# The last row tile's 512 output columns in two groups, and its last store in two halves

## The chip, the cores and the metric

The kernel runs on one core of one Trainium2 chip. The metric is device time in microseconds (us) of one execution. Before the change three executions took 163.49, 163.81 and 164.55 us; the median is 163.81.

## What is computed

A gated feed-forward layer: with x of 2048 x 640, w_gate and w_up of 640 x 1536, and w_down of 1536 x 640, all in bf16,

```python
def reference(x, w_gate, w_up, w_down):
    g = _silu(x @ w_gate)
    u = x @ w_up
    return (g * u) @ w_down
```

## The kernel before

The 2048 rows of x go through in four blocks of 512 (`sb`). For each block and each of twelve slices of 128 of the inner 1536 columns (`fc`), TensorE (PE) makes the gate and the up product in two PSUM tiles (`proj`, L192, five matmuls each), ScalarE (ACT) takes the silu of one (L212), and VectorE (DVE) multiplies it by the other into `aT` (L213), which holds the inner activations with the inner dimension on the partitions.

Then the block's output is made. The 640 output columns are split at `DA` = 512. The last 128 columns come first, transposed (`po_t`, L263, 512 rows wide, turned back by DVE at L274 and stored by ACT's queue at L276); in the last block this covers only the first three row tiles. The first 512 columns follow in four row tiles of 128 rows (`j` = 0 to 3): twelve matmuls of 512 columns each accumulate in `po_a` (L288), ACT casts the tile to bf16 (`ot`, L296), and SP issues the store (L301). In the very last row tile (`sb` = 3, `j` = 3, called `last`) the remaining 128 columns are made straight, not transposed: twelve matmuls of 128 columns into `po_b` (L305), a cast by DVE into `ot_b` (L313), and a store issued by ACT (L314).

`po_a` has two PSUM slots and `ot` three buffers, so a row tile waits for the cast of the tile two before it, and its cast for the store of the tile three before it. Beside this DVE works through 96 dot products for the last four rows (`row_dots`, L145); `do_dots` spreads them over the kernel, and `row_tail` at the first row tile of the last block finishes them, so none are left in the last row tile.

The Tile framework places the waits. On DVE and SP the program order is kept as it is written (`keep_order`); on ACT and PE it comes out in program order at the end as well. `_trim` takes away the barriers at the end: SP alone waits there for every semaphore (L394), two per EVENT_SEMAPHORE instruction and the last one on a DRAIN, and then clears them.

Of the kernel before, what the change touches and what calls it, by code (L numbers as in the profile page):

```python
# [10 lines left out]
def _body(  # L11
# [8 lines left out]
    nc = tc.nc  # L20
    P = nc.NUM_PARTITIONS
    f32 = mybir.dt.float32
    bf16 = mybir.dt.bfloat16
# [3 lines left out]
    B, S0, D = x.shape  # L27
# [3 lines left out]
    out2 = out.rearrange("b s d -> (b s) d")  # L31

    KD = D // P
    KF = F // P
    S_BLK = 512
    NSB = S // S_BLK
    SUB = S_BLK // P
    DA = 512
# [4 lines left out]
    ROW_J = 0  # L43
# [5 lines left out]
    outp = ctx.enter_context(tc.tile_pool(name="outp", bufs=3))  # L49
    psum = ctx.enter_context(  # L50
        tc.tile_pool(name="psum", bufs=2, space=bass.MemoryType.PSUM)
    )
# [6 lines left out]
    wd_sb = consts.tile([P, KF, D], bf16)  # L59
    aT = consts.tile([P, KF, S], bf16)  # L60
# [62 lines left out]
    def turn_x(sb):  # L123
        s_sl = slice(sb * S_BLK, (sb + 1) * S_BLK)
        nc.sync.dma_start_transpose(out=xT[:, :, s_sl], in_=xt_v[s_sl])

    def turn_w(dst, src):
        for a in range(0, KF, WT_STEP):
            nc.sync.dma_start_transpose(
                out=dst[:, a : a + WT_STEP, :], in_=src[:, a : a + WT_STEP, :]  # L130
            )
# [3 lines left out]
        out=x_row[:],  # L135
        in_=x2[S - T : S, :].rearrange("t d -> (t d)").partition_broadcast(P),
# [19 lines left out]
    def row_tail():  # L156
        for _ in dots:
            pass
        nc.scalar.activation(row_s[:], row_g[:], ACT.Silu)
        nc.vector.tensor_tensor(  # L160
            out=aT[:, :, S - T : S], in0=row_s[:], in1=row_u[:], op=ALU.mult
        )
# [3 lines left out]
    def do_dots(n):  # L166
        for _ in range(n):
            next(dots, None)
# [21 lines left out]
    def proj(ps, w_sb, fc, sb, c0, c1, cols=lambda ap: ap):  # L190
        for kd in range(KD):
            nc.tensor.matmul(  # L192
                cols(ps[:, c0:c1]),
                lhsT=w_sb[:, kd, fc * P : (fc + 1) * P],
                rhs=cols(xT[:, kd, sb * S_BLK + c0 : sb * S_BLK + c1]),
                start=(kd == 0),
                stop=(kd == KD - 1),
            )
# [4 lines left out]
    def gu_tiles():  # L203
        pg = psum.tile([P, S_BLK], f32, tag="gu", name="pg", bufs=4)
        pu = psum.tile([P, S_BLK], f32, tag="gu", name="pu", bufs=4)
        return pg, pu

    def gate(pg, pu, sb, fc, n_s):

        s0 = sb * S_BLK  # L210
        sg = work.tile([P, S_BLK], f32, name="sg")
        nc.scalar.activation(sg[:, 0:n_s], pg[:, 0:n_s], ACT.Silu)  # L212
        nc.vector.tensor_tensor(  # L213
            out=aT[:, fc, s0 : s0 + n_s], in0=sg[:, 0:n_s], in1=pu[:, 0:n_s], op=ALU.mult
        )
# [31 lines left out]
    for sb in range(NSB):  # L247
        n_s = S_BLK if sb < NSB - 1 else S_BLK - T
        for fc in range(KF):
            if sb == 0 and fc < 2:  # L250
                continue
            pg, pu = gu_tiles()
            proj(pg, wg_sb, fc, sb, 0, n_s)
            proj(pu, wu_sb, fc, sb, 0, n_s)
            gate(pg, pu, sb, fc, n_s)
            if sb > 0 and fc < KF - 2:
                do_dots(2)


        n_t = (SUB if sb < NSB - 1 else SUB - 1) * P  # L260
        po_t = psum.tile([P, n_t], f32, tag="po_b", name="po_t")
        for kf in range(KF):
            nc.tensor.matmul(  # L263
                po_t[:],
                lhsT=wd_sb[:, kf, DA:D],
                rhs=aT[:, kf, sb * S_BLK : sb * S_BLK + n_t],
                start=(kf == 0),
                stop=(kf == KF - 1),
            )
        ot_t = outp.tile([P, n_t], bf16, name="ot_t")  # L270
        ot_q = outp.tile([P, n_t], bf16, name="ot_q")
        nc.scalar.copy(ot_t[:], po_t[:])  # L272
        do_dots(3)
        nc.vector.transpose(out=ot_q[:], in_=ot_t[:])  # L274
        for q in range(P // Q):
            nc.scalar.dma_start(  # L276
                out=out2[
                    sb * S_BLK : sb * S_BLK + n_t, DA + q * Q : DA + (q + 1) * Q
                ].rearrange("(i r) c -> r i c", r=Q),
                in_=ot_q[q * Q : (q + 1) * Q, :].rearrange("r (i c) -> r i c", c=Q),  # L280
            )

        for j in range(SUB):
            s0 = sb * S_BLK + j * P
            last = sb == NSB - 1 and j == SUB - 1
            po_a = psum.tile([P, DA], f32, tag="po_a", name="po_a")
            for kf in range(KF):
                nc.tensor.matmul(  # L288
                    po_a[:],
                    lhsT=aT[:, kf, s0 : s0 + P],  # L290
                    rhs=wd_sb[:, kf, 0:DA],
                    start=(kf == 0),
                    stop=(kf == KF - 1),
                )
            ot = outp.tile([P, DA], bf16, name="ot")
            nc.scalar.copy(ot[:], po_a[:])  # L296
            if 0 < j:
                do_dots(3)
            if sb == NSB - 1 and j == ROW_J:
                row_tail()  # L300
            nc.sync.dma_start(out=out2[s0 : s0 + P, 0:DA], in_=ot[:])  # L301
            if last:
                po_b = psum.tile([P, D - DA], f32, tag="po_b", name="po_b")
                for kf in range(KF):
                    nc.tensor.matmul(  # L305
                        po_b[:],
                        lhsT=aT[:, kf, s0 : s0 + P],
                        rhs=wd_sb[:, kf, DA:D],
                        start=(kf == 0),
                        stop=(kf == KF - 1),  # L310
                    )
                ot_b = outp.tile([P, D - DA], bf16, name="ot_b")
                nc.vector.tensor_copy(out=ot_b[:], in_=po_b[:])  # L313
                nc.scalar.dma_start(out=out2[s0 : s0 + P, DA:D], in_=ot_b[:])  # L314
        if sb == 0:
            turn_x(2)
            turn_w(wuT, wut_v)
            turn_x(3)
# [72 lines left out]
def kernel(tc, *args):  # L391
    _body(tc, *args)
    tc.close()
    tc.compile()  # L394
    _trim(tc.nc)
# [30 lines left out]
```

## Time and profile before

| what | value |
|---|---|
| median of three executions | 163.81 us |
| the profiled execution: its span, first to last instruction (the page gives it no other time) | 163.0 us |
| PE busy | 159.9 us, 98% |
| DVE busy | 111.7 us, 69% |
| ACT busy | 42.6 us, 26% |
| granted TensorE clock | 1.000 |
| matmul spacing at 512 columns | 0.216 us |
| last matmul ends | 160.94 us |
| last DMA issue (`ot_b`) | 161.28 us |
| cast of 128x512 by ACT | 585 ns |
| cast of 128x128 by DVE | 290 ns |

Times in the profile count from the first instruction. The median is 0.81 us longer than the span; the span leaves out what the device does before the first and after the last instruction. A DMA is issued by an engine's queue (SPq, ACTq) and then takes a while to land, which is when its semaphore is complete; the time of a landing is not busy time of any engine. Lines are called L and a number; DMA issues have a queue, a count, the KB of each and the median us from issue to landing.

### The profile page before, as it was taken

Reading aid. Unit: us, or ns where it says so; the run is one execution under the profiler, and the core shown is the slowest. Engines: PE = TensorE matmul, PEld = TensorE weight load, DVE = VectorE, ACT = ScalarE, POOL = GpSimd, SP = SyncE. Lnnn points to the kernel's source line nnn. Section 1 sums busy time; section 2 is a strip of 40 time slices with the busy share of each in tenths; the row PEclk is TensorE's granted clock in tenths of the full one; section 3 lists DMA queues with packets and bytes.
Section 4 is the critical chain, followed back from the end, with each engine's and each line's share of the span. In section 5 each row is a group of like instructions: output and inputs, shape, how many; then the busy total and the mean of one; then the engine's idle time right before and its main releaser. Section 6 shows DMA issues by size and latency. Waiting matters only on the chain.

```text
span 163.0 us, 2109 instructions
## 1 busy us (share of the span) xinstructions
PE 159.9 (98%) x787; PEld 77.1 (47%) x799; DVE 111.7 (69%) x251; ACT 42.6 (26%) x73; POOL 0.6 (0%) x6
## 2 busy tenths in 40 slices
PE   9999999999999999999999999999999999999994
PEld 8764444444444444444444444444444444445442
DVE  2133333399559999979919999979964999993000
ACT  3142222212132222222222322221214222222121
POOL 1000000000000000000000000000000000000000
PEclk9999999999999999999999999999999999999999
DMA  7999999993169995003210000000420000000312
GB/s 206 269 342 354 362 229 250 214 198 61 64 123 153 249 186 131 0 0 33 65 64 0 4 0 2 0 0 0 64 68 32 0 0 0 0 4 0 53 35 72
DMA packets 42585, 15.86 MB, mean 97 GB/s; under 512 B 34512, under 2 KB 42448, under 8 KB 42576
## 3 DMA queue, kind: packets, MB, share of 16 engines
q1 hardware_dynamic: 33680, 14.88, 37.0%
q10 hardware_dynamic: 8896, 0.85, 3.8%
q8 instruction: 6, 0.10, 0.2%
q14 instruction: 3, 0.02, 0.1%
HBM read 7.21 MB, written 2.62 MB: 60 GB/s over the span
## 4 chain that ended last, share of the span: by engine, by line
PE 98%; issue 1%; DVE 0%
PE pg L192 32%; PE pu L192 32%; PE po_a L288 25%; PE po_t L263 6%; PE pw L174 2%; PE pt L183 1%; PE po_b L305 0%; DVE ot_b L313 0%; DVE ones L104 0%
## 5 line engine op out<-in xcount | busy, mean ns | idle before, releaser
L192 PE MATMUL pg<-xT,wg_sb 128*128 128x512 bf16 (+4 forms) x248 | 60.3, 370 | 0.4
L192 PE MATMUL pu<-xT,wu_sb 128*128 128x512 bf16 (+3 forms) x250 | 59.9, 370 | 0.0
L213 DVE TENSOR_TENSOR aT<-sg,pu 128x512 bf16<-128x512 f32 (+1 forms) x48 | 32.7, 682 | 29.3 <-PE pu L192 27.9
L212 ACT ACTIVATE sg<-pg 128x512 f32<-128x512 f32 (+1 forms) x48 | 28.6, 596 | 67.4 <-PE pg L192 62.7
L288 PE MATMUL po_a<-wd_sb,aT 128*128 128x512 bf16 x188 | 41.7, 379 | 0.2
L145 DVE SCALAR_TENSOR_TENSOR prod<-wgT,x_row 128x640 f32<-128x640 bf16 x48 | 39.4, 820 | 1.1
L145 DVE SCALAR_TENSOR_TENSOR prod<-wuT,x_row 128x640 f32<-128x640 bf16 x48 | 39.4, 821 | 1.0
L192 PEld LDWEIGHTS <-wg_sb 128*128 128x128 bf16 x255 | 25.0, 100 | 27.6
L192 PEld LDWEIGHTS <-wu_sb 128*128 128x128 bf16 x250 | 24.1, 98 | 27.4
L288 PEld LDWEIGHTS <-aT 128*128 128x128 bf16 x192 | 18.8, 98 | 22.5
L296 ACT CAST ot<-po_a 128x512 bf16<-128x512 f32 x16 | 9.4, 585 | 32.4 <-PE po_a L288 20.7
L263 PE MATMUL po_t<-aT,wd_sb 128*128 128x512 bf16 (+1 forms) x47 | 10.3, 366 | 0.1
L263 PEld LDWEIGHTS <-wd_sb 128*128 128x128 bf16 x48 | 4.7, 98 | 5.1
L313 DVE CAST ot_b<-po_b 128x128 bf16<-128x128 f32 x1 | 0.3, 290 | 9.9 <-PE po_b L305 9.9
L188 DVE COPY xT<-pt 128x640 bf16<-128x640 bf16 (+1 forms) x4 | 1.7, 423 | 6.4 <-PE pt L183 6.4
L272 ACT CAST ot_t<-po_t 128x512 bf16<-128x512 f32 (+1 forms) x4 | 2.2, 558 | 11.6 <-PE po_t L263 11.6
L145 DVE DVE_READ_ACCUMULATOR prod<-wgT,x_row 128x1 f32 x48 | 3.9, 81 | 0.0
L145 DVE DVE_READ_ACCUMULATOR prod<-wuT,x_row 128x1 f32 x48 | 3.9, 81 | 0.0
L274 DVE STREAM_TRANSPOSE ot_q<-ot_t 128x512 bf16<-128x512 bf16 (+1 forms) x4 | 2.7, 678 | 1.7 <-ACT ot_t L272 1.7
L174 PE MATMUL pw<-ones 128*128 128x128 bf16 x22 | 2.9, 313 | 0.4 <-DVE ones L104 0.4
L174 PEld LDWEIGHTS <-ones 128*128 128x128 bf16 x22 | 2.4, 148 | 0.4 <-DVE ones L104 0.4
L183 PE MATMUL pt<-ident,x_sb 128*128 128x128 bf16 x20 | 2.4, 289 | 0.0
(15 smaller groups left out, 7.2 us busy)
## 6 DMA issues: line engine op xcount, KB each, us to landing
out_dram<-ot SPq DMA_DIRECT2D x16, 128.0 KB, 1.7
wd_sb<-in_w_down_dram SPq DMA_DIRECT2D x1, 1920.0 KB, 13.1
wg_sb<-in_w_gate_dram SPq DMA_DIRECT2D x2, 640.0 KB, 7.3
wu_sb<-in_w_up_dram SPq DMA_DIRECT2D x2, 640.0 KB, 8.4
x_row<-in_x_dram SPq DMA_DIRECT2D x1, 640.0 KB, 4.7
x_sb<-in_x_dram SPq DMA_DIRECT2D x3, 160.0 KB, 2.9
out_dram<-ot_q ACTq DMA_DIRECT2D x12, 32.0 KB, 2.0
wg_sb<-in_w_gate_dram SPq DMA_DIRECT2D x1, 320.0 KB, 4.9
```

Source lines behind the costliest of these rows:

```text
L145: nc.vector.scalar_tensor_tensor(out=prod[:], in0=wT[:, fc, :], scalar=1.0, in1=x_row[:, t, :], op0=ALU.mult, op1=ALU.mult, accum_out=acc[ ...
L174: nc.tensor.matmul(pw[:, 0:P], lhsT=ones[:], rhs=ones[:], start=True, stop=True)
L183: nc.tensor.transpose(out=pt[:, kd - k0, :], in_=x_sb[:, c, kd * P : (kd + 1) * P], identity=ident[:],)
L188: copy(out=xT[:, k0:k1, c_sl], in_=pt[:])
L192: nc.tensor.matmul(cols(ps[:, c0:c1]), lhsT=w_sb[:, kd, fc * P : (fc + 1) * P], rhs=cols(xT[:, kd, sb * S_BLK + c0 : sb * S_BLK + c1]), st ...
L212: nc.scalar.activation(sg[:, 0:n_s], pg[:, 0:n_s], ACT.Silu)
L213: nc.vector.tensor_tensor(out=aT[:, fc, s0 : s0 + n_s], in0=sg[:, 0:n_s], in1=pu[:, 0:n_s], op=ALU.mult)
L263: nc.tensor.matmul(po_t[:], lhsT=wd_sb[:, kf, DA:D], rhs=aT[:, kf, sb * S_BLK : sb * S_BLK + n_t], start=(kf == 0), stop=(kf == KF - 1),)
L272: nc.scalar.copy(ot_t[:], po_t[:])
L274: nc.vector.transpose(out=ot_q[:], in_=ot_t[:])
L288: nc.tensor.matmul(po_a[:], lhsT=aT[:, kf, s0 : s0 + P], rhs=wd_sb[:, kf, 0:DA], start=(kf == 0), stop=(kf == KF - 1),)
L296: nc.scalar.copy(ot[:], po_a[:])
```

## The change

In the last row tile the 512 columns are made as two groups of 256, each with its own PSUM tile (both of tag `po_a`), its own twelve matmuls, its own cast by ACT into its own `ot` buffer, and its own store on SP. The 128 columns after them keep their twelve matmuls and their cast by DVE, but the store is split by rows: rows 0 to 63 are issued by ACT, rows 64 to 127 by SP. All other row tiles run as before. On PE this makes twelve matmuls and twelve weight loads more, on ACT one cast more, on SP two DMA issues more; the order of everything else on every engine stays as it is.

```diff
-            po_a = psum.tile([P, DA], f32, tag="po_a", name="po_a")
-            for kf in range(KF):
-                nc.tensor.matmul(
-                    po_a[:],
...
-            ot = outp.tile([P, DA], bf16, name="ot")
-            nc.scalar.copy(ot[:], po_a[:])
-            if 0 < j:
-                do_dots(3)
-            if sb == NSB - 1 and j == ROW_J:
-                row_tail()
-            nc.sync.dma_start(out=out2[s0 : s0 + P, 0:DA], in_=ot[:])
+            cols = [(0, DA, "po_a")]
             if last:
-                po_b = psum.tile([P, D - DA], f32, tag="po_b", name="po_b")
+                cols = [(0, DA // 2, "po_a"), (DA // 2, DA, "po_a"), (DA, D, "po_b")]
+            for c0, c1, tag in cols:
+                po = psum.tile([P, c1 - c0], f32, tag=tag, name="po_a")
                 for kf in range(KF):
                     nc.tensor.matmul(
-                        po_b[:],
+                        po[:],
                         lhsT=aT[:, kf, s0 : s0 + P],
-                        rhs=wd_sb[:, kf, DA:D],
+                        rhs=wd_sb[:, kf, c0:c1],
...
-                ot_b = outp.tile([P, D - DA], bf16, name="ot_b")
-                nc.vector.tensor_copy(out=ot_b[:], in_=po_b[:])
-                nc.scalar.dma_start(out=out2[s0 : s0 + P, DA:D], in_=ot_b[:])
+                ot = outp.tile([P, c1 - c0], bf16, name="ot" if c1 < D else "ot_b")
+                if c1 < D:
+                    nc.scalar.copy(ot[:], po[:])
+                    stores = [(nc.sync, 0, P)]
+                else:
+                    nc.vector.tensor_copy(out=ot[:], in_=po[:])
+                    stores = [(nc.scalar, 0, P // 2), (nc.sync, P // 2, P)]
+                if 0 < j and not last:
+                    do_dots(3)
+                if sb == NSB - 1 and j == ROW_J:
+                    row_tail()
+                for eng, r0, r1 in stores:
+                    eng.dma_start(out=out2[s0 + r0 : s0 + r1, c0:c1], in_=ot[r0:r1, :])
```

More of the change, by code (lines that the diff above doesn't have):

```diff
@@ L285, in _body @@
             last = sb == NSB - 1 and j == SUB - 1
-            po_a = psum.tile([P, DA], f32, tag="po_a", name="po_a")
-            for kf in range(KF):
-                nc.tensor.matmul(
-                    po_a[:],
[L290 to L294, printed above, removed]
-            ot = outp.tile([P, DA], bf16, name="ot")
-            nc.scalar.copy(ot[:], po_a[:])
-            if 0 < j:
-                do_dots(3)
-            if sb == NSB - 1 and j == ROW_J:
-                row_tail()
-            nc.sync.dma_start(out=out2[s0 : s0 + P, 0:DA], in_=ot[:])
+            cols = [(0, DA, "po_a")]
             if last:
-                po_b = psum.tile([P, D - DA], f32, tag="po_b", name="po_b")
+                cols = [(0, DA // 2, "po_a"), (DA // 2, DA, "po_a"), (DA, D, "po_b")]
+            for c0, c1, tag in cols:
+                po = psum.tile([P, c1 - c0], f32, tag=tag, name="po_a")
                 for kf in range(KF):
                     nc.tensor.matmul(
-                        po_b[:],
+                        po[:],
                         lhsT=aT[:, kf, s0 : s0 + P],
-                        rhs=wd_sb[:, kf, DA:D],
+                        rhs=wd_sb[:, kf, c0:c1],
                         start=(kf == 0),
```

## The prediction

> **What bounds the kernel now.** I read first the shares of the chain that ended last, then that chain's last stretch in order of time, then the instructions of the last microseconds, the closing waits of SP, and the DMA activity behind them.
>
> The page's part 4 gives the chain by engine and by line:
>
> ```profile
> PE 98%; issue 1%; DVE 0%
> ```
>
> TensorE is the bound almost to the end. No matmul work is taken away here, so a gain can come only from what follows the last matmul. The chain from 157 us on (start, length, what):
>
> ```profile
> 156.80 3.45 PE po_a L288 x16
> 160.25 0.68 PE po_b L305 x12
> 160.94 0.02 issue
> 160.96 0.29 DVE ot_b L313
> ```
>
> The chain stops at 161.25, while the span is 163.0. The rest is the final stores. The timeline of the end (start, length, engine and line):
>
> ```profile
> 160.33 0.58 ACT L296 CAST ot<-po_a 128x512 bf16<-128x512 f32 x1 [2.05 <-PE po_a L288]
> 160.96 0.29 DVE L313 CAST ot_b<-po_b 128x128 bf16<-128x128 f32 x1 [9.85 <-PE po_b L305]
> 161.28 0.36 ACTq L314 DMA_DIRECT2D out_dram<-ot_b  x1
> ```
>
> SP issues the 512-column store at 160.94 (0.33 us, SP's timeline), before ACT issues the 128-column one at 161.28. How long both take to land, from the DMA issues of the window 161 to 163 (KB, us from issue to landing):
>
> ```profile
> out_dram<-ot SPq DMA_DIRECT2D x1, 128.0 KB, 1.8
> out_dram<-ot_b ACTq DMA_DIRECT2D x1, 32.0 KB, 1.6
> ```
>
> So `ot` lands at about 160.94 + 1.76 = 162.70 and `ot_b` at 161.28 + 1.59 = 162.87 (the second decimals are the landing records of the trace). SP's closing instructions agree:
>
> ```profile
> L394 SPq EVENT_SEMAPHORE  x5: 28/28/1205, 161.3 to 162.8; - x5
> L394 SPq DRAIN  x1: 13/13/13, 162.9 to 162.9; - x1
> L394 SPq EVENT_SEMAPHORE_RANGE_CLEAR  x1: 52/52/52, 162.9 to 162.9; - x1
> ```
>
> The 1205 ns is the wait that ends with `ot` (162.72). One more semaphore pair follows, then the DRAIN at 162.89, 0.02 after `ot_b` landed, and the end 0.11 later. The store that ends the kernel is `ot_b`, with `ot` 0.17 ahead. The two share the DMA engines (columns: stretch, then busy time by engine, PE clock, DMA share, GB/s):
>
> ```profile
> 161.80:162.00 0.20, 0.00 (x0) 0.00 (x0) 0.00 (x0) 0.00 (x0) 0.00 (x0) 1.00 0.89 292
> 162.00:162.20 0.20, 0.00 (x0) 0.00 (x0) 0.00 (x0) 0.00 (x0) 0.00 (x0) 1.00 1.01 323
> 162.20:162.40 0.20, 0.00 (x0) 0.00 (x0) 0.00 (x0) 0.00 (x0) 0.00 (x0) 1.00 0.78 167
> 162.40:162.60 0.20, 0.00 (x0) 0.00 (x0) 0.00 (x0) 0.00 (x0) 0.00 (x0) 1.00 0.02 3
> ```
>
> The engines are full from 161.8 to 162.4, then quiet, and `ot_b` is not landed until 162.87: of its 1.59 us, 0.88 goes before its first packet, 0.28 is packets, and 0.43 is between the last packet and the last of its sixteen semaphore steps.
>
> **Part by part.** The sum is against the profiled execution's span, 163.0; the page gives it no other time. The median of the runs, 163.81, lies 0.81 above, and I carry that over.
>
> *Matmuls.* Twelve of 512 columns become 24 of 256, with twelve more weight loads. Spacing: 3.45/16 = 0.216 us at 512 columns, 0.68/12 = 0.057 at 128. On the line through both, 256 columns take 0.110, so 24 take 2.64 at these rounded figures and 2.62 with the start records (0.2158, 0.0559), against 2.59. Bounds: half of a 512 gives 24 x 0.108 = 2.59, or nothing; two of a 128 give 24 x 0.112 = 2.69, or +0.10. I take +0.03. The twelve loads are hidden: at L305 a load and a 128-column matmul together advance every 0.057 us, so a load fits under 0.110. If that cover failed, they would cost the 0.098 of the weight-load row each, 1.2 us.
>
> *PSUM slot.* The second group gets the slot of row tile 2, whose cast ran 157.70 to 158.28. Its first matmul comes about 1.31 us after 157.5 to 157.7, near 158.9 to 159.0: 0.6 us of cover. Were it late, the rest of the row tile would wait behind it on PE. In front, the first group's slot and the `ot` buffers (stores that landed 155.35 and 157.43) are long free.
>
> *Casts.* ACT's 585 ns for 512 columns and 478 ns for 384 (`ot_t`) give 371 ns for 256; nothing in the trace is that cast, but the 128x256 COPY at L188 took 372. The first group's runs under the second's matmuls. The second runs from 160.33 + 0.03 to 160.73 instead of 160.92.
>
> *Stores.* Group one goes out on SP near 159.4, lands near 161.1, and meets nobody. Group two is issued near 160.76, with half the bytes in as many packets; between the 1.59 and 1.70 of the `ot_b` and `ot` rows, it lands at 162.35 to 162.46. SP is free at 161.09, so the second half of `ot_b`, now queued behind it on SP, finds its data late (DVE ends at 161.28), not its queue: 0.19 us of cover. Behind the half's issue on SP stand only the closing waits. ACT and SP issue the halves side by side at 161.31.
>
> *The halves' landing.* No row shows 16 KB. Lower end: half of the 0.28 of packets goes (-0.14), and the crowding with `ot` goes (`ot_b` lagged 0.43 behind its last packet, lone `ot` stores 0.36: -0.08), so 1.37. Upper end: two transfers that finish together also finish their semaphore steps one after another. Just this shows now: `ot`'s sixteen steps run from 162.47 to 162.70 and `ot_b`'s from 162.67 to 162.87, some 12 ns each with hardly an overlap. A second set of sixteen costs 0.17: 1.76. The nearest row is the present 1.59, and I take 1.60: crowding with `ot` is exchanged for crowding between halves.
>
> The Trainium skill, "DMA: Bandwidth & Descriptors", under "Rules for kernel authors", says of two transfers to disjoint partition halves that they serialize on the same sixteen engines, and advises one transfer of 128 partitions. The full windows above agree that two queues share engines; no run here yet shows two halves. By that rule alone the packets would give back nothing, and the sum below would lose its lower end.
>
> *Closing.* Eleven semaphores are still to be waited for, in pairs, but now one half's sits in the pair ahead of the DRAIN and the other's on the DRAIN. If both land together, the step from pair to DRAIN (0.106 from pair end to DRAIN start now, partly waiting; 0.04 between the idle pairs) stands behind the landing: 0 to +0.10. I take +0.03.
>
> *Sum.* +0.03 (PE) + 0.01 (landing) + 0.03 (closing) = +0.07: span 163.07, time 163.88, given as 163.9. Ends: +0.00 - 0.22 + 0.00 = -0.22, so 163.6; +0.10 + 0.17 + 0.10 = +0.37, so 164.2.
>
> **Rivals.**
> *The tail shortens.* Halves land as light, uncrowded transfers, at 1.37 to 1.50. For: the engine share falls to nothing between `ot`'s earlier end and the halves. Against: 1.3 of the 1.59 us is not packets. 163.6 to 163.75, say 163.65.
> *Completions queue up (slower).* Place: the 32 semaphore steps of the two halves, then SP's pair and DRAIN. Price: 0.17 for the sixteen steps more, +0.10 for the pair. It decides as soon as both halves' first steps come within 0.2 us of each other, which equal issue times make likely; against it, the first steps of smaller transfers can begin sooner. 164.05 to 164.2.
> *An instruction fetch under a final store.* In the window 118.2 to 120.2 the queue of instruction loads moved one packet, 1.39 us long, and a store then in flight took the longest landing of its line, 3.7 us instead of 1.7. PE's stream is now 24 instructions longer. Price +2.0: 165.8. Against: these fetches come every 27 us (91.9, 118.8, 146.2), the next near 173, and 24 instructions move that by less than their 2.6 us of matmuls.
> *Nothing changes,* because the change leaves issue-to-landing alone: 163.81, inside the forecast.
>
> **How the numbers follow.** Forecast, within 0.15 of no change: 0.5. Shorter tail: 0.24. Queued completions: 0.22. Fetch or another stall of over 1.6 us: 0.03. Faster by over 1% needs 1.64 us out of the 2.06 between the last matmul and the end, where one landing alone takes 1.4 or more: 0.01. One per cent is about what a measurement of this kernel can tell from no change. So 0.01 faster, 0.96 same, 0.03 slower. The range takes the ends of the sum, 163.6 and 164.2, widened by 0.3 on either side because the three runs before already lie 163.49 to 164.55: 163.3 to 164.5.
>
> **What would show it.** Right: 256-column matmuls every 0.108 to 0.112 us; casts of 0.37; the last cast's store issued near 160.76; both halves issued within 0.05 of 161.31; span 162.8 to 163.4. Halves landing in under 1.5 us speak for the shorter tail, over 1.7 for queued completions. Wrong would be: idle time on PE before the second group, one half issued late on SP, halves on fewer engines (a packet phase longer than 0.3 us), or a last store of 3 us.

## The result, and the profile after

The changed kernel takes 165.01 us (median), the kernel before 163.95 on the same chip; the ratio is 1.0038, with a 95% interval from 1.0021 to 1.0054. By the ratio that is slower by 0.62 us, or between 0.34 and 0.89; the two medians lie further apart, 1.06 us, which is taken up again further down. The forecast was +0.07, its upper end +0.37. Measured again later beside other kernels, the ratio was 1.0023 (0.9999 to 1.0047).

The span of the profiled execution went from 163.0 to 163.7 us. The end of the timeline of the changed kernel (start, length, engine and line):

```profile
159.23 0.37 ACT L301 CAST ot<-po_a 128x256 bf16<-128x256 f32 x1 [0.77 <-PE po_a L292]
160.54 0.37 ACT L301 CAST ot<-po_a 128x256 bf16<-128x256 f32 x1 [0.94 <-PE po_a L292]
161.17 0.29 DVE L304 CAST ot_b<-po_a 128x128 bf16<-128x128 f32 x1 [9.88 <-PE po_a L292]
161.49 0.55 SPq L311 DMA_DIRECT2D out_dram<-ot_b  x1
161.49 0.57 ACTq L311 DMA_DIRECT2D out_dram<-ot_b  x1
```

The two halves are issued at the same moment, as foretold, but each issue takes 0.55 to 0.57 us, where the whole store took 0.36. From issue to landing (DMA issues of the window from 161.3 on):

```profile
out_dram<-ot_b SPq DMA_DIRECT2D x1, 16.0 KB, 1.8
out_dram<-ot_b ACTq DMA_DIRECT2D x1, 16.0 KB, 2.0
```

Half the bytes need 1.79 and 2.03 us, where the whole needed 1.59. What the DMA engines do meanwhile (columns: stretch, then busy time by engine, PE clock, DMA share, GB/s):

```profile
161.80:162.00 0.20, 0.00 (x0) 0.00 (x0) 0.00 (x0) 0.00 (x0) 0.00 (x0) 1.00 0.88 254
162.00:162.20 0.20, 0.00 (x0) 0.00 (x0) 0.00 (x0) 0.00 (x0) 0.00 (x0) 1.00 0.20 54
162.20:162.40 0.20, 0.00 (x0) 0.00 (x0) 0.00 (x0) 0.00 (x0) 0.00 (x0) 1.00 0.00 0
162.40:162.60 0.20, 0.00 (x0) 0.00 (x0) 0.00 (x0) 0.00 (x0) 0.00 (x0) 1.00 0.00 0
162.60:162.80 0.20, 0.00 (x0) 0.00 (x0) 0.00 (x0) 0.00 (x0) 0.00 (x0) 1.00 0.35 58
162.80:163.00 0.20, 0.00 (x0) 0.00 (x0) 0.00 (x0) 0.00 (x0) 0.00 (x0) 1.00 0.27 46
163.00:163.20 0.20, 0.00 (x0) 0.00 (x0) 0.00 (x0) 0.00 (x0) 0.00 (x0) 1.00 0.35 60
```

Up to 162.2 it is the second group's store. Then the engines stand idle for half a microsecond with both halves already issued. Before the change they were full from 161.8 to 162.4 without a break. The halves' packets come in two separate lots: SP's start from 162.67 to 162.89 and ACT's from 162.94 to 163.16 (packet records). The first ones come 1.19 and 1.45 us after the issue, where the whole store's first packet came after 0.88. The data itself is no slower: each half's packets take 0.23 us, the whole store's took 0.28. The transfers start late.

SP's closing waits:

```profile
L391 SPq EVENT_SEMAPHORE  x5: 28/28/946, 162.1 to 162.6; - x5
L391 SPq DRAIN  x1: 13/13/13, 163.6 to 163.6; - x1
L391 SPq EVENT_SEMAPHORE_RANGE_CLEAR  x1: 52/52/52, 163.6 to 163.6; - x1
```

The 946 ns are the wait for ACT's half, which lands at 163.53.

The 0.70 us between the two spans has three parts. By the start records, the last row tile begins 0.18 later already; the change is not in force there, and where this comes from is told with the first experiment. The last row tile's matmuls take 0.03 more. From the end of DVE's cast to the end of the span it is 2.24 us instead of 1.75: +0.49. The last two parts, 0.52, belong to the change, and 0.52 lies inside the interval from 0.34 to 0.89. **That last stretch, from the end of DVE's cast to the end of the span, is the measure of all that follows**, since it leaves out the spread of the rest. I call it the tail.

### The profile page after: what moved, and what is told of

Its sections match the earlier page's. It is cut to its first block, busy times and chain, and to the rows that moved or that the text cites. A ratio compares the mean times of both kernels' runs of the same rounds, so it can differ in the third digit from the quotient of the medians.

```text
span 163.7 us, 2139 instructions
## 1 busy us (share of the span) xinstructions
PE 160.1 (98%) x799; PEld 78.4 (48%) x811; DVE 111.8 (68%) x251; ACT 42.8 (26%) x74; POOL 0.6 (0%) x6
## 4 chain that ended last, share of the span: by engine, by line
PE 98%; issue 1%; DVE 0%
PE pg L192 32%; PE pu L192 32%; PE po_a L292 26%; PE po_t L263 6%; PE pw L174 2%; PE pt L183 1%; DVE ot_b L304 0%; DVE ones L104 0%
## 5 line engine op out<-in xcount | busy, mean ns | idle before, releaser
L292 PE MATMUL po_a<-wd_sb,aT 128*128 128x512 bf16 (+2 forms) x212 | 42.4, 358 | 0.2
L292 PEld LDWEIGHTS <-aT 128*128 128x128 bf16 x216 | 20.7, 98 | 21.6
L301 ACT CAST ot<-po_a 128x512 bf16<-128x512 f32 (+1 forms) x17 | 9.5, 560 | 32.0 <-PE po_a L292 20.2
```

What stands on the lines that cost most here:

```text
L292: nc.tensor.matmul(po[:], lhsT=aT[:, kf, s0 : s0 + P], rhs=wd_sb[:, kf, c0:c1], start=(kf == 0), stop=(kf == KF - 1),)
L301: nc.scalar.copy(ot[:], po[:])
```

## The experiments

Three theories stood against each other. Theory 1: issues that ACT and SP make at the same moment hold each other up. Theory 2: a transfer of 64 rows is slow to issue by itself; later it is divided into 2a, every count of rows other than 128 is slow, and 2b, only 64 is. Theory 3: the groups of 256 columns cost the time.

### The kernel before, once more

No edit.

> The kernel before, unchanged, so that its spans can be set beside its times. All theories: ratio 1.000 within 0.2%; from the end of DVE's last cast to the end of the span 1.75 us; `ot_b` lands 1.59 after its issue. If the time lies 1.3 us above the span here too, as in the changed kernel, then the 0.81 of the prediction compared a profile with runs other than its own.

Ratio 0.9995 (0.9975 to 1.0015). The tail was 1.72 us, the landing of `ot_b` 1.57. The profiled execution took 164.78 us with a span of 163.4, so 1.38 us lie outside the span; in the kernel's other executions it was 1.3 as well. The 0.81 of the prediction was therefore not a property of the kernel: by the 1.3, the span of 163.0 was that of an execution of about 164.3 (an estimate, its own time is not on record), set beside a median of three others.

This unchanged kernel had spans from 162.3 to 163.4. In the profiles the spread comes from the first ten microseconds: the same weight load of `wg_sb` came at 9.8 us in the first profile of before, at 10.0 here, at 9.0 in the last kernel below, and behind it the same PE stream runs on at one pace, but for a few tenths. The 0.18 of the result is of this kind. Windows 6 to 9 us of this kernel, and then of the last one below (PE, PEld, DVE, ACT, POOL, each with the count of its instructions, then PE clock, DMA share, GB/s):

```profile
6.00:9.00 3.00, 3.00 (x24) 1.92 (x22) 0.36 (x1) 0.37 (x1) 0.00 (x0) 1.00 0.95 252
```

```profile
6.00:9.00 3.00, 3.00 (x36) 2.35 (x35) 0.36 (x2) 1.00 (x3) 0.00 (x0) 1.00 0.94 258
```

Twenty-four matmuls against 36 in the same three microseconds, though the code up to there is the same and the PE clock column reads 1.00 in both. The start records show how: a 128-column matmul starts every 0.107 us at first and every 0.056 us later, and the pace changes at about 6.4 us here, at about 4.3 in the last kernel. Two microseconds more at half the pace are one microsecond, and the first `po_a` matmul starts 1.06 us later here (34.24 against 33.18). In the first profiles of before and of the changed kernel the pace changes at about 6.0 and 6.2, and the first `po_a` matmul starts at 34.02 and 34.20. What sets the moment was not looked into.

### The groups alone

```diff
-                    stores = [(nc.scalar, 0, P // 2), (nc.sync, P // 2, P)]
+                    stores = [(nc.scalar, 0, P)]
```

> Two groups of 256 columns, but the 128-column store whole, from ACT. Theory 1 (issues that ACT and SP make at the same moment hold each other up): nothing is issued beside it, so the issue takes 0.36 us again, the first packet comes 0.82 to 0.88 after it, and it lands in 1.45 to 1.60; cast end to span end 1.60 to 1.75; ratio 0.999 to 1.001. Theory 2 (a transfer of 64 rows is itself slow): the same. Theory 3 (the groups themselves cost: 24 matmuls, two casts, two stores): the tail stays near 2.2 and the ratio at 1.003.

Ratio 1.0005 (0.9985 to 1.0025), tail 1.63 us. The store's issue and landing (duration in ns; then us):

```profile
L311 ACTq DMA_DIRECT2D out_dram<-ot_b x1: 363/363/363, 161.0 to 161.0; - x1
...
DMA to landing us min/median/max: 1.5/1.5/1.5
```

Theory 3 falls. The tail is even shorter by about 0.1: the last store lands after 1.48 instead of 1.59 and 1.57. The packets of the store ahead of it now end 0.22 before its own begin, which is the likely reason. The groups give 0.03 of it back on PE.

### The halves alone

```diff
-                cols = [(0, DA // 2, "po_a"), (DA // 2, DA, "po_a"), (DA, D, "po_b")]
+                cols = [(0, DA, "po_a"), (DA, D, "po_b")]
```

> One group of 512 columns as before, the 128-column store in halves on ACT and SP. Theory 1: SP is just done with the 512-column issue, so the halves go out together again, issues of 0.55 to 0.57, the later half landing about 2.0 us after its issue; cast end to span end 2.2; ratio 1.003 (1.002 to 1.005). Theory 2: the same tail. Theory 3: ratio 1.000, tail 1.75.

Ratio 1.0018 (0.9999 to 1.0037), tail 2.22 us.

```profile
L311 ACTq DMA_DIRECT2D out_dram<-ot_b x1: 563/563/563, 161.3 to 161.3; - x1
L311 SPq DMA_DIRECT2D out_dram<-ot_b x1: 551/551/551, 161.4 to 161.4; - x1
...
DMA to landing us min/median/max: 1.8/1.9/2.0
```

The whole loss of the tail is there without the groups. This run can't tell theory 1 from theory 2.

### The halves one after the other on one queue

```diff
-                    stores = [(nc.scalar, 0, P // 2), (nc.sync, P // 2, P)]
+                    stores = [(nc.scalar, 0, P // 2), (nc.scalar, P // 2, P)]
```

> Two groups, halves, but both halves issued by ACT one after the other. Theory 1: each issue takes 0.33 to 0.36 again and each half lands 1.45 to 1.6 after its own issue, the second issued 0.36 to 0.40 later; cast end to span end 2.0 to 2.1; ratio about 1.002. Theory 2: each half still takes 1.8 to 2.0 from its own issue, so cast end to span end 2.3 to 2.5; ratio 1.004 to 1.005.

Ratio 1.0047 (1.0024 to 1.0070), tail 2.57 us.

```profile
L311 ACTq DMA_DIRECT2D out_dram<-ot_b x2: 535/567/599, 160.9 to 161.5; - x2
...
DMA to landing us min/median/max: 1.8/1.8/1.8
```

Here SP issues nothing near the halves, and still the first one takes 0.535 us to issue, has its first packet after 1.18, and lands after 1.77. That is close to theory 2's 1.8 to 2.0 and not theory 1's 1.45 to 1.6; the tail is a little longer than theory 2's 2.3 to 2.5. The two issues side by side in the changed kernel had pointed to theory 1.

### The price of a store by its rows

Stores of the second and third block's row tiles in pieces, one list for each row tile, `(queue, first row, end row, columns)`. First the rows' number:

```diff
...
-            nc.sync.dma_start(out=out2[s0 : s0 + P, 0:DA], in_=ot[:])
+            for eng, r0, r1, c0, c1 in PARTS.get((sb, j), [("sync", 0, P, 0, DA)]):
+                getattr(nc, eng).dma_start(
+                    out=out2[s0 + r0 : s0 + r1, c0:c1], in_=ot[r0:r1, c0:c1]
+                )
```

> A look at the price of one store by its number of rows, away from the end: the kernel before, with the stores of the second and third block's row tiles cut into pieces: 64+64 rows, 4x32, two of 128 rows by 256 columns, 96+32, 64+64 on two queues, 112+16, four of 128 rows by 128 columns, 64+64 rows of 128 columns with 128x384. Whole stores of 128 rows have an issue of 0.33 us and a first packet 0.82 after it. Theory 2 (the row count sets it): every piece of 64 rows, on either queue, of 256 or 1024 bytes a row, has an issue of 0.53 to 0.60 and a first packet 1.15 to 1.25 after it, and pieces of 128 rows keep 0.33 and 0.82 whatever their columns. Theory 2a: all counts other than 128 (16, 32, 96, 112) are slow too; theory 2b: only 64 is. Theory 1 (issues at the same moment): all pieces but those issued on two queues at once keep 0.33 to 0.36. The stores are hidden, so the time should stay within 0.3% of before under all theories.

Timeline of SP's queue, at the first piece of four row tiles: 64 rows; 128 rows by 256 columns; 96 rows; 64 rows by 128 columns:

```profile
77.07 0.56 SPq L314 DMA_DIRECT2D out_dram<-ot  x1
...
81.03 0.35 SPq L314 DMA_DIRECT2D out_dram<-ot  x1
...
83.67 0.33 SPq L314 DMA_DIRECT2D out_dram<-ot  x1
...
122.47 0.47 SPq L314 DMA_DIRECT2D out_dram<-ot  x1
```

Pieces of 64 rows took 0.47 to 0.60 to issue whatever their width and queue, and their first packet came 1.13 to 1.25 after the issue. One came later still: of two 64-row pieces issued at the same moment by SP and ACT, SP's had its first packet after 1.13 and ACT's after 1.43. 96 and 112 rows cost what whole stores of 128 cost (0.32 to 0.33, first packet 0.82). Pieces issued right behind another took 0.42 to 0.44 with 16, 32 or 128 rows. Right behind a 64-row piece it was 0.59 to 0.60, for two more pieces of 64 rows and also for one of 128 rows, so a 64-row store holds up what its queue issues next. By the first pieces of the row tiles, theory 2a falls and 2b stands. The one execution took 164.31 us, inside the spread of before.

### Where the 64 rows begin

The same frame with other lists: 64 rows from row 32, 48+80, 32+96, 16+112, 80+48, every second row, two separate column pieces of each of 64 rows, and once more 64 rows on ACT beside 64 on SP.

```diff
...
-    (1, 0): [("sync", 0, 64, 0, 512), ("sync", 64, 128, 0, 512)],
-    (1, 1): [("sync", r, r + 32, 0, 512) for r in range(0, 128, 32)],
+    (1, 0): [("sync", 32, 96, 0, 512), ("sync", 0, 32, 0, 512), ("sync", 96, 128, 0, 512)],
+    (1, 1): [("sync", 0, 48, 0, 512), ("sync", 48, 128, 0, 512)],
...
+    (2, 0): [("sync", 0, 80, 0, 512), ("sync", 80, 128, 0, 512)],
+    (2, 1): [("sync", 0, 128, 0, 512, 2), ("sync", 1, 128, 0, 512, 2)],
+    (2, 2): [("sync", 0, 64, 0, 512, 1, 2), ("sync", 64, 128, 0, 512)],
...
```

> A second look at the price of one store by its rows: the kernel before, with row tiles of the second and third block cut as 64 rows from row 32 (then 32+32), 48+80, 32+96, 16+112, 80+48, 64+64 as every second row, 64 rows as two pieces of 2x128 separate columns (then 64), and 64 on ACT beside 64 on SP. Theory 2b: pieces of 64 rows take an issue of 0.47 to 0.60 wherever they begin, all others as first of a tile 0.32 to 0.36 and behind another 0.42 to 0.44. If what counts is a start at row 0 or 64, or 4 rows for each of the 16 DMA engines in a row, the pieces from row 32 or of every second row, or the two-dimensional ones, fall back to 0.33.

SP's queue at the first piece of seven row tiles: 64 rows from row 32; 48 rows; 32; 16; 80; 64 as every second row; 64 rows of two separate column pieces.

```profile
76.44 0.63 SPq L322 DMA_DIRECT2D out_dram<-ot  x1
...
78.25 0.36 SPq L322 DMA_DIRECT2D out_dram<-ot  x1
80.72 0.31 SPq L322 DMA_DIRECT2D out_dram<-ot  x1
83.35 0.31 SPq L322 DMA_DIRECT2D out_dram<-ot  x1
115.15 0.32 SPq L322 DMA_DIRECT2D out_dram<-ot  x1
116.98 0.53 SPq L322 DMA_DIRECT2D out_dram<-ot  x1
119.57 0.67 SPq L320 DMA_DIRECT2D out_dram<-ot  x1
```

All the 64-row pieces are slow, wherever they begin and however they are spaced; 16, 32, 48 and 80 rows are not. One piece of 32 rows also took 0.57, right behind a 64-row one. The pair of 64 rows on two queues took 0.49 (SP) and 0.54 (ACT) to issue, with first packets after 1.14 and 1.46. The one execution took 163.69 us. Why 64 is dear was not found: it is neither the bytes, nor the queue, nor the starting row.

### The last store in two halves of 64 columns

```diff
-                    stores = [(nc.scalar, 0, P // 2), (nc.sync, P // 2, P)]
+                    stores = []
+                    for eng, h0, h1 in ((nc.scalar, c0, c0 + 64), (nc.sync, c0 + 64, c1)):
+                        eng.dma_start(out=out2[s0 : s0 + P, h0:h1], in_=ot[:, h0 - c0 : h1 - c0])
```

> Two groups; the last store in two halves of 64 columns, each of all 128 rows, ACT and SP at the same moment. Theory 2: 128 rows, so the issues take 0.33 to 0.37, first packets 0.82 to 0.9 after them, both land in 1.45 to 1.70; cast end to span end 1.65 to 1.85; ratio 0.999 to 1.002. Theory 1: issues of 0.5 or more and cast end to span end of 2.1 or more; ratio 1.003 or more.

Ratio 1.001 (0.999 to 1.003), tail 1.79 us.

```profile
L307 SPq DMA_DIRECT2D out_dram<-ot_b x1: 332/332/332, 161.1 to 161.1; - x1
L307 ACTq DMA_DIRECT2D out_dram<-ot_b x1: 377/377/377, 161.1 to 161.1; - x1
...
DMA to landing us min/median/max: 1.4/1.5/1.6
```

Two queues at the same moment, and no slow issue. Theory 1 falls as the main cause. What is left of it is small: the first packets come 0.08 apart, and the later of the two lands 0.17 after the other.

### The last store cut at row 96

```diff
-                    stores = [(nc.scalar, 0, P // 2), (nc.sync, P // 2, P)]
+                    stores = [(nc.scalar, 0, 96), (nc.sync, 96, P)]
```

> The changed kernel with its last store cut at row 96 instead of row 64: 96 rows from ACT, 32 from SP, at the same moment. Theory 2b (a piece of exactly 64 rows is what is slow to issue): issues of 0.32 to 0.43, first packets 0.8 to 0.95 after them, both landed in 1.45 to 1.65; cast end to span end 1.65 to 1.80; ratio 0.999 to 1.002. If cutting by rows as such were slow: issues near 0.55, cast end to span end 2.1 or more, ratio 1.003 or more.

Ratio 1.0012 (0.9989 to 1.0034), tail 1.77 us.

```profile
L311 SPq DMA_DIRECT2D out_dram<-ot_b x1: 346/346/346, 161.4 to 161.4; - x1
L311 ACTq DMA_DIRECT2D out_dram<-ot_b x1: 378/378/378, 161.4 to 161.4; - x1
...
DMA to landing us min/median/max: 1.4/1.5/1.6
```

Moving the cut by 32 rows takes 0.46 us off the changed kernel's tail, the cleanest test of theory 2b. (The times, 1.0012 and 1.0023 with wide intervals, are too coarse to show it.) Beside it ran the changed kernel itself:

> The changed kernel itself once more, beside the others on one chip: cast end to span end 2.2 to 2.3, ratio 1.002 to 1.005.

Ratio 1.0023 (0.9999 to 1.0047), tail 2.23, issues of 0.55 and 0.57 again.

### The whole last store on SP

```diff
-                    stores = [(nc.scalar, 0, P // 2), (nc.sync, P // 2, P)]
+                    stores = [(nc.sync, 0, P)]
```

> Two groups, the 128-column store whole, from SP in place of ACT. SP's 128-row stores have their first packet 0.82 to 0.83 after the issue, ACT's 0.86 to 0.88; SP has to finish the issue of the second group's store first, which it has (0.19 us of cover). Cast end to span end 1.57 to 1.65 against 1.63 with ACT; not to be told apart in the time.

One execution of 163.80 us: tail 1.60 us, the store lands 1.45 after its issue. It is the shortest tail of all, so it was timed:

> The variant with two groups and the whole last store on SP, timed: its end from DVE's cast on was 1.60 us in its profile against 1.75 and 1.72 before, and its matmuls cost 0.03 more, so 0.09 to 0.12 us should be gained, a ratio of 0.9993; an interval of 0.2% either way can't tell that from no change, but it excludes 1.003 if the halves alone were the cost.

Ratio 1.0006 (0.9984 to 1.0029), tail 1.60 again. No version was shown to be faster than the kernel before: a tail shorter by 0.12 to 0.15 us, less 0.03 on PE, is 0.05 to 0.07% and drowns in the interval. Its interval does exclude 1.003.

## Why the prediction was wrong

That the change is worth less than one per cent was foretold. That it makes the kernel slower was forecast only barely, with +0.07 and a chance for the shorter tail (0.24) as large as for the queued completions (0.22). The size was not foretold, and the time lies outside the range.

**The step that failed** is "The halves' landing": "No row shows 16 KB ... The nearest row is the present 1.59, and I take 1.60", with 1.37 to 1.76 as ends. Measured: 1.79 and 2.03. In choosing the row I went by bytes, and let the time from issue to first packet (0.88) be the same for any store. It is not: with 64 rows the issue takes 0.2 us longer and the first packet comes 0.3 to 0.4 later, which the runs by row count show. On top, the later of two halves lands after the earlier: by 0.25 in the changed kernel, and by 0.17 and 0.20 in the two cuts that have no 64 rows. In those two cuts the first packets come only 0.08 and 0.04 apart; in all five pairs of 64-row stores on two queues (the changed kernel twice, the halves alone, and one pair in each of the two kernels with stores in pieces) they come 0.26 to 0.33 apart. So a weaker form of theory 1 holds for 64-row stores: two of them do hold each other up, ahead of the first packet. No row of the trace of before held a store of 64 rows, so it could not be read there; but the upper end was built from semaphore steps and packets alone, and never asked what a different shape does to the issue.

**The baseline** was a second and smaller miss. "The median of the runs, 163.81, lies 0.81 above, and I carry that over" set the span of one execution beside the median of others; in the executions of the timed kernels, which show both, the distance is 1.26 to 1.42. The forecast hangs on the median, though, and not on the span: in the twelve executions of the result the median before was 163.95, so this cost 0.14.

**The rest is not shown to be the change's.** From the forecast of 163.88 to the median of 165.01 it is 1.13 us. The baseline gives 0.14, and the 0.52 of the trace is 0.45 more than the +0.07. The remaining half a microsecond is in neither the trace nor the ratio. Eight of the changed kernel's twelve executions took 164.95 to 165.19; when it was run again, the medians lay only 0.55 apart (164.57 against 164.02). The likely reason is the spread, since the first ten microseconds alone moved two profiles 1.06 us apart. Added to 163.95, the 0.52 of the trace gives 164.47, just inside the range, so the landing and this rest took the time out of it together.

Of the other steps:
- *Matmuls, +0.03*: right. The row of 256-column matmuls and that of the casts, in the changed kernel's groups by shape from 157 us on:

```profile
L292 PE MATMUL po_a<-wd_sb,aT 128*128 128x256 bf16 x24 | 2.8, 273 | 0.0
...
L301 ACT CAST ot<-po_a 128x256 bf16<-128x256 f32 x2 | 0.7, 372 | 1.7 <-PE po_a L292 1.7
```

  They start every 0.109 us with no idle time ahead of them; the weight loads are hidden, and the second group found its PSUM slot free.
- *Casts*: 371 ns foretold, 372 measured.
- *Stores of the groups*: issued where foretold (160.94, less the 0.18 of the later start, is 160.76). The second landed after 1.54, a little under the 1.59 to 1.70 that I gave; it met nobody.
- *Issue of the halves*: at 161.49, which is 161.31 and the 0.18.
- *Closing*: from the last landing to the end 0.17 instead of 0.13, so +0.04 where I took +0.03.
- *Rival "completions queue up"*: right in sign, wrong in cause; a landing over 1.7, which was to speak for it, came from something else. SP's half has its sixteen semaphore steps from 163.10 to 163.27 and ACT's from 163.34 to 163.53; they do not queue, since the packets were already apart.
- *Rival "the tail shortens"*: true of the groups (tail 1.63 and 1.60 against 1.75 and 1.72), seen in no split of the last store (1.77 and more).
- *Rival "instruction fetch"*: the fetch came at 118.8 and 119.0 in the two kernels and none came at the end.
- *The rule of the Trainium skill*, "DMA: Bandwidth & Descriptors", under "Rules for kernel authors", that halves by partitions serialize on the same engines, points the right way: the lots of packets follow each other here. At row 96 the packets of the two pieces overlapped, and the later landed 0.20 behind. The rule prices the split at no gain; the loss of half a microsecond comes on top of it. The prediction said that by this rule alone the sum would lose its lower end; without the packets' 0.14 the crowding's 0.08 would still have been left in it.

## What to carry to other kernels

At the end of this kernel a store of 32 KB costs 1.4 to 1.6 us from issue to landing, of which only 0.26 to 0.28 is data, so splitting it saved nothing, and the extra on the issue side was paid in full. Before cutting a transfer, measure the issue and the first packet of the new shape somewhere off the critical path: in one run, eight row tiles gave the price of eight shapes. And set a span beside the time of its own execution only.

## What the runs showed of the hardware that I had not expected

- A store of exactly 64 rows from SBUF took 0.47 to 0.67 us to issue and 1.1 to 1.3 to its first packet (1.4 to 1.5 for the later of two at the same moment). As the first of a row tile, 16, 32, 48, 80, 96, 112 and 128 rows took 0.31 to 0.36 and 0.81 to 0.85 on SP; one first piece of 32 rows, 0.19 us behind a 64-row one, took 0.44. The slowness of 64 rows held on both queues, for rows of 256 and 1024 bytes, from rows 0, 32 and 64, and for every second row.
- The next store on the queue is slow to issue too: 0.57 for 32 rows and 0.59 for 128 rows right behind a 64-row store, against 0.42 to 0.44 behind other shapes.
- The same kernel's span differed by 1.1 us from one execution to the next (162.3 to 163.4). Between two profiles 1.4 us apart, 1.06 of it was there before the first `po_a` matmul, from the moment at which PE's pace doubled (6.4 and 4.3 us).
- The device time lies 1.26 to 1.42 us above the span in all executions of the timed kernels, and 1.71 and 1.49 in the single executions of the two kernels with stores in pieces; why these two differ is not shown.
